# Attention with stationary values and per-head 64-row scores, in a fused attention and two-layer MLP kernel

## The chip, the cores and the metric

The kernel runs on one core of a Trainium2 chip. The metric is the device time of one execution in microseconds (us), as the median of several runs. A core has TensorE (PE, matrix products into PSUM), VectorE (DVE), ScalarE (ACT), GpSimd (POOL) and SyncE (SP, which issues the DMAs). Each works through its own queue in order and waits there on semaphores. PSUM has eight banks of 512 fp32 numbers per partition.

## The reference

For 8 batches and 8 heads, 576 queries of 64 numbers meet 72 keys and values, each the mean of 8 neighbours. Then come two layers on 4608 tokens.

```python
def _attn_ref(q, k, v):
    k_p = k.reshape(B, H, Sp, pool, D).mean(axis=3)
    v_p = v.reshape(B, H, Sp, pool, D).mean(axis=3)
    scores = scale * np.matmul(q, k_p.transpose(0, 1, 3, 2))
    scores = scores - np.max(scores, axis=-1, keepdims=True)
    attn = np.exp(scores)
    attn = attn / (np.sum(attn, axis=-1, keepdims=True) + 1e-09)
    return np.matmul(attn, v_p)

def _moe_ref(x, w_in, w_out, g_ln):      # 512 -> 1024 -> 512
    h = x @ w_in
    solu = h * softmax(h)
    ln = (solu - mean(solu)) / np.sqrt(var(solu) + 1e-06) * g_ln
    return ln @ w_out

def _moe2_ref(x, w_in, w_out):           # 512 -> 2048 -> 512
    h = x @ w_in
    g = h * (1.0 / (1.0 + np.exp(-1.702 * h)))
    return g @ w_out
```

## The kernel before

The program has two parts. The first computes the attention and the first layer for 36 tiles of 128 tokens, and meanwhile turns the weights of the second layer into sums of blocks in fp16, which go to DRAM. The second part computes the second layer in 12 blocks of 384 tokens with a seven-product scheme; the change leaves it as it is.

In the first part every piece of work is a Python generator that yields operations: `keys` and `values` (per batch), `attention` (per tile), `Pair.hidden` (per tile), `Pair.norm` and `Pair.project` (per pair of tiles), `Quarter.run` and `unit_scale` (second-layer weights). A planner (`Plan.run`) keeps an estimate of when each engine is free, asks every generator for its next operation, and emits the one with the earliest start, shifted a little by due times. So the order on each engine is fixed when the program is built, and it moves when an operation's estimated cost (`cost`, `T`, `X`), a buffer count or the operations change. An operation made with `VG` may go to POOL or DVE; the planner prefers POOL until DVE would be done over 3 us earlier. All operations of this part are recorded at L470 (engines), L491 (DMAs), L499 (products) and L514 (transposes on PE); their tiles tell them apart.

One tile of `attention` goes as follows. `qt` comes in with two heads stacked in its 128 partitions, in four pairs. The scores of a pair are one fp32 product of `qt` with `kbd`, in which the keys of the two heads stand in diagonal blocks with zeros beside them (144 columns); `keys` scales them into it from `kp`. In the records an fp32 product is two passes on PE. The eight heads' scores lie in two banks, `psx`. DVE takes the maxima (`mx`) and subtracts them (`e`); ACT takes exp. ACT and then POOL write `e` as fp16 high part and remainder into `st`, and a transposing DMA gives `aT`. The product with the values has `aT` as stationary operand and streams 65 columns of `vst`: a column of ones and the 64 values of a head, so it gives the sum of the exponentials as well. DVE adds 1e-9, takes the reciprocal (`rs`) and scales the result into `x`. PE transposes `x` in four products (L514), and ACT and DVE write the high part and the remainder of that into `xT`.

`psx` is one buffer of two banks: scores, value products, transposes and some of the spreads of a maximum over partitions (`largest`) take turns in it. `psh` (hidden products, two buffers of two banks) and `psy` (projections, two buffers of one bank) fill the other six. A tile of 128 tokens that straddles two batches has its products in two parts of 64 tokens.

`Pair.norm` takes small DVE operations on 128x2 numbers (`q`, `v`, `a`) around one POOL operation (`r`), then writes `zs`, which a transposing DMA turns into `zT` for `project`, whose result goes through ACT (`y`) to DRAM.

Of the kernel before, what the change touches and what calls it, by code (L numbers as in the profile page):

```python
# [8 lines left out]
F32 = mybir.dt.float32  # L9
# [3 lines left out]
ALU = mybir.AluOpType  # L13
# [18 lines left out]
VW = D + 1  # L32
PAD = 16
VP = P + PAD
# [42 lines left out]
V_TOP = 2.0 ** 14  # L77
LN_UP = 2.0 ** 10
# [198 lines left out]
def moe_kernel(ctx: ExitStack, tc: tile.TileContext, qT, kT, vT, w_in, w_out, g_ln, w2_in, w2_out, eye, outT):  # L277
# [135 lines left out]
    with ExitStack() as ph:  # L413
# [7 lines left out]
        psy = ph.enter_context(tc.tile_pool(name="psy", bufs=2, space=PSUM))  # L421
# [3 lines left out]
        vst = [wp.tile([P, H * VP + PAD], F16, name=f"vst{i}") for i in range(2)]  # L425
        kbd = [wp.tile([P, NPAIR, 2 * SP], F32, name=f"kbd{i}") for i in range(2)]
# [69 lines left out]
        def T(products):  # L496
# [9 lines left out]
            c = sum(count(p[2]) * 0.417 + 3 if p[2].dtype == F16 else count(p[2]) * 1.667 + 6 for p in products)  # L506
# [17 lines left out]
        def largest(am, alln, least, early=True):  # L524
# [8 lines left out]
            if early:  # L533
                ps = yield New(psy, [P, 2, YB], F32, "psy", "psy", 2)
            else:
                ps = yield New(psx, [P, 2, 512], F32, "psx", "psx")
            yield T([(ps[:, 0, :P], ones, diag, True, True)])
            drop(diag)
            yield V("tensor_reduce", out=alln, in_=ps[:, 0, :P], axis=AX.X, op=ALU.max)
# [207 lines left out]
        def pooled(kind, b, src, due):  # L747
            yield lambda: b == 0 or begun[kind][b - 1] == 2
            dst = yield New(kv, [P, NPAIR, SP], F32, kind + "p", bufs=1)
            yield until(*[start(half(kind, b, j, src, dst), due + j) for j in range(2)])  # L750
            return dst
# [12 lines left out]

        def values(b, due):
            vp = yield from pooled("v", b, vT, due)
# [15 lines left out]
            yield D(  # L782
                vst[b % 2][:, 0 : H * VP].rearrange("p (g w) -> p g w", w=VP)[:, :, PAD:VP], vx.rearrange("p a k -> p (a k)"),
                turn=True,
            )
# [17 lines left out]
        def attention(t):  # L803
# [5 lines left out]
            if t < 2:  # L809
# [3 lines left out]
            yield there(qt, *(kbd[b % 2] for _, _, b in spans(t)))  # L813
# [11 lines left out]
                    for o, n, b in spans(t)  # L825
                ]
# [7 lines left out]
            if plan.free["act"] + ACT_SPARE < plan.free["dve"]:  # L834
                for h in range(H):
                    yield A(out=e[:, h], in_=s4[:, h // 4, h % 4], func=AF.Exp, bias=mx[:, h : h + 1])
                drop(ps)
            else:
# [5 lines left out]
                yield A(out=e, in_=e, func=AF.Exp)  # L844
# [13 lines left out]
            x = yield New(sb, [P, DM], F32, "x", bufs=2)  # L858
            ps = yield New(psx, [P, 2, 512], F32, "psx", "psx")
            def v_at(h, c):  # L860
                return (h // 2 * 2 + c) * VP + PAD - 1 + h % 2 * VW

            p4 = ps.rearrange("p b (a c) -> p (b a) c", a=2)
# [3 lines left out]
                        p4[o : o + n, h // 2, (h % 2) * VW : (h % 2 + 1) * VW],  # L867
# [617 lines left out]
```

## Time and profile before

| what | value |
|---|---|
| time, median of 3 runs (lowest, highest) | 1304.92 us (1303.19, 1305.73) |
| profiled execution: its own time, its span | 1300.56 us, 1298.8 us |
| busy over the span: PE, DVE, ACT, POOL | 89%, 64%, 56%, 47% |
| first part, up to the last `psy` product | 589.2 us |
| mean granted TensorE clock | 0.987 of full |

Busy time counts an instruction from its start to its end on the engine, with what it waits for there after it has started. The 1.8 us between the span and the execution's own time lie outside the first and last instruction.

### The profile page before, as it was taken

Reading aid. Unit: us, or ns where it says so; the run is one execution under the profiler, and the core shown is the slowest. Engines: PE = TensorE matmul, PEld = TensorE weight load, DVE = VectorE, ACT = ScalarE, POOL = GpSimd, SP = SyncE. Lnnn points to the kernel's source line nnn. Section 1 sums busy time; section 2 is a strip of 40 time slices with the busy share of each in tenths; the row PEclk is TensorE's granted clock in tenths of the full one; section 3 lists DMA queues with packets and bytes.
Section 4 is the critical chain, followed back from the end, with each engine's and each line's share of the span. In section 5 each row is a group of like instructions: output and inputs, shape, how many; then the busy total and the mean of one; then the engine's idle time right before and its main releaser. Section 6 shows DMA issues by size and latency. Waiting matters only on the chain.

```text
span 1298.8 us, 27820 instructions
## 1 busy us (share of the span) xinstructions
PE 1160.4 (89%) x11822; PEld 1006.1 (77%) x11822; DVE 829.4 (64%) x1364; ACT 730.8 (56%) x961; POOL 606.8 (47%) x516
## 2 busy tenths in 40 slices
PE   2658878988889899989999999999999999999998
PEld 2334655666566667679999999999999999999998
DVE  8999989989889784424554637364554637273633
ACT  5578766767777775444453636354453636364543
POOL 5564577757775764323342426152332415252431
PEclk9969999999999999989999999999999999999999
DMA  9878899999979759557010101101010101101000
GB/s 306 243 211 185 206 241 264 223 243 245 252 200 217 174 126 256 182 98 268 14 38 15 36 26 32 44 8 44 14 38 14 38 26 29 47 7 44 12 16 26
DMA packets 246526, 152.88 MB, mean 118 GB/s; under 512 B 163585, under 2 KB 226177, under 8 KB 244097
## 3 DMA queue, kind: packets, MB, share of 16 engines
q1 hardware_dynamic: 246400, 151.09, 44.8%
q8 instruction: 93, 1.52, 0.5%
q14 instruction: 33, 0.26, 0.1%
HBM read 77.66 MB, written 33.55 MB: 86 GB/s over the span
## 4 chain that ended last, share of the span: by engine, by line
PE 26%; POOL 10%; DVE 9%; ACT 8%; issue 3%; DMA 0%; ACTq 0%; SPq 0%; POOLq 0%
PE bank_a L1295 17%; PE bank_d L1295 7%; DVE g L1342 6%; ACT w_g L1330 6%; POOL w_g L332 3%; POOL w_g L331 3%; POOL w_g L329 2%; PE bank_b L1295 2%; POOL w_g L330 2%; PE psy L499 1%; ACT g L1339 1%; DVE c L1308 1%; DVE w_g L329 1%; DVE w_g L330 1%; DVE w_g L331 0%
## 5 line engine op out<-in xcount | busy, mean ns | idle before, releaser
L1295 PEld LDWEIGHTS <-w2i 128*128 128x128 f16 x4032 | 334.2, 98 | 29.0 <-issue 28.9
L1295 PEld LDWEIGHTS <-w2o 128*128 128x128 f16 x4032 | 333.9, 98 | 8.8 <-issue 8.2
L1295 PE MATMUL bank_a<-ys,w2i 128*128 128x192 f16 x2304 | 213.7, 246 | 23.0 <-ACT c L1305 21.0
L329 POOL TENSOR_TENSOR w_g<-w_g 128x384 f32<-128x384 f32 x36 | 43.8, 1217 | 377.9 <-ACT w_g L1330 377.9
L499 PE MATMUL psh<-w1i,xT 128*128 128x512 f16 x864 | 206.3, 389 | 3.4 <-DVE mean L470 3.4
L1295 PE MATMUL bank_a<-g,w2o 128*128 128x192 f16 x2304 | 205.7, 246 | 1.2
L499 PE MATMUL psy<-zT,w1o 128*128 128x256 f16 x1728 | 198.9, 275 | 5.4 <-ACT tt L470 3.8
L499 PEld LDWEIGHTS <-w1o 128*128 128x128 f16 x1728 | 169.1, 99 | 27.0 <-issue 4.2
L1342 DVE SCALAR_TENSOR_TENSOR g<-w_g,gu_b,g 128x1152 f16<-128x1152 f32 (+1 forms) x96 | 168.1, 1772 | 25.4 <-ACT g L1339 25.3
L499 PEld LDWEIGHTS <-xT 128*128 128x128 f16 x864 | 85.0, 100 | 94.0 <-issue 11.8
L1305 ACT ACTIVATE c<-bank_a 128x384 f32<-128x384 f32 x192 | 91.5, 484 | 112.1 <-PE bank_a L1295 111.0
L1339 ACT ACTIVATE g<-w_g,gu_b 128x1152 f16<-128x1152 f32 (+1 forms) x96 | 132.9, 1407 | 38.2 <-POOL w_g L332 37.9
L1308 DVE SCALAR_TENSOR_TENSOR c<-bank_d,c 128x384 f32<-128x384 f32 x96 | 53.3, 555 | 132.3 <-ACT c L1305 97.8
L470 POOL TENSOR_TENSOR zs<-tt,zs 128x1024 f16<-128x1024 f32 x36 | 77.2, 2146 | 75.6 <-ACT zs L470 74.8
L1295 PE MATMUL bank_d<-g,w2o 128*128 128x192 f16 x1152 | 102.7, 246 | 3.6 <-DVE g L1342 3.6
L1295 PE MATMUL bank_d<-ys,w2i 128*128 128x192 f16 x1152 | 104.9, 246 | 0.0
L1330 ACT ACTIVATE w_g<-c,ch_b 128x1536 f32<-128x1536 f32 x48 | 75.3, 1568 | 37.0 <-DVE c L1308 36.9
L1305 ACT ACTIVATE c<-bank_a,co_b 128x384 f32<-128x384 f32 x47 | 26.8, 571 | 107.2 <-PE bank_a L1295 107.2
L499 PE MATMUL psx<-kbd,qt 128*128 128x144 f32 (+1 forms) x320 | 46.6, 307 | 25.5 <-DMA qt<-qT 12.3
L1308 DVE SCALAR_TENSOR_TENSOR c<-bank_b,c 128x384 f32<-128x384 f32 x48 | 26.7, 556 | 66.0 <-PE bank_b L1295 45.4
L470 POOL TENSOR_TENSOR lo<-w_f,hi 128x512 f16<-128x512 f32 (+1 forms) x47 | 63.6, 1366 | 7.2 <-DMA w2o_dram<-lo 4.0
L499 PEld LDWEIGHTS psx<-kbd,qt 128*128 128x128 f32 (+1 forms) x320 | 41.7, 194 | 31.8 <-DVE raw_z L470 12.3
(183 smaller groups left out, 1745.7 us busy)
## 6 DMA issues: line engine op xcount, KB each, us to landing
raw<-w_out SPq DMA_DIRECT2D x12, 1024.0 KB, 6.7
raw<-w_in SPq DMA_DIRECT2D x10, 1024.0 KB, 7.8
half<-kT SPq DMA_DIRECT2D x16, 576.0 KB, 5.3
half<-vT SPq DMA_DIRECT2D x16, 576.0 KB, 5.4
qt<-qT SPq DMA_DIRECT2D x36, 256.0 KB, 3.7
y_dram<-y SPq DMA_DIRECT2D x36, 256.0 KB, 2.7
y<-y_dram SPq DMA_DIRECT2D x48, 192.0 KB, 3.3
outT<-c SPq DMA_DIRECT2D x48, 192.0 KB, 1.9
```

The source lines that it names most:

```text
L329: eng.tensor_tensor(out=w[:, 1], in0=q[:, Q12], in1=q[:, Q11], op=ALU.subtract)
L330: eng.tensor_tensor(out=w[:, 2], in0=q[:, Q22], in1=w[:, 1], op=ALU.subtract)
L331: eng.tensor_tensor(out=w[:, 0], in0=q[:, Q22], in1=q[:, Q12], op=ALU.subtract)
L332: eng.tensor_tensor(out=w[:, 3], in0=q[:, Q21], in1=w[:, 2], op=ALU.subtract)
L470: getattr(eng, name)(*args, **kw)
L499: nc.tensor.matmul(*p[:3], start=p[3], stop=p[4])
L1295: nc.tensor.matmul(bank[:, q], self.weight(p, q, kk, w), self.data(p, kk, i), start=(first and q == 0 and kk == 0 and w == 0 and i == 0), ...
L1305: nc.scalar.activation(out=self.c[:, i], in_=bank, func=AF.Copy, scale=self.scale)
L1308: nc.vector.scalar_tensor_tensor(out=self.c[:, i], in0=bank, scalar=self.scale, in1=self.c[:, i], op0=ALU.mult, op1=ALU.add)
L1330: nc.scalar.activation(out=self.w[:, 0:4], in_=self.c, func=AF.Gelu_apprx_sigmoid, scale=self.ch)
L1339: nc.scalar.activation(out=self.g[:, 0, s], in_=self.w[:, s], func=AF.Copy, scale=self.gu)
L1342: nc.vector.scalar_tensor_tensor(out=self.g[:, 1, s], in0=self.w[:, s], scalar=self.gu, in1=self.g[:, 0, s], op0=ALU.mult, op1=ALU.subtract,)
```

## The change

The scores no longer use diagonal keys. `keys` sums the pooled keys straight into two alternating tiles `kps`, unscaled, and the scale goes into the exponential. Each head's scores are a product of its own 64 partitions of `qt` and `kps` with 72 columns; even heads write the first bank of `psx`, odd heads the second. So there are 8 products of 72 columns where there were 4 of 144.

The normalisation moves ahead of the value product: DVE sums `e` over the keys, adds 1e-9 and scales by 2^-14, takes the reciprocal, and POOL or DVE multiplies `e` by it. The value product now has 64 columns of `vst` as stationary operand and streams the 128 tokens of `aT`; even heads fill partitions 0 to 63 of the result, odd heads 64 to 127, so that the result already stands transposed. `x`, its scaling from PSUM, and the four transposes on PE are gone, and so are the columns of ones and the padding of `vst`. `xT` is read from the new one-bank buffer `psv`, scaled by 2^-14. `psv` also takes the later spreads of `largest`. To make room, `psy` has one buffer instead of two. In the planner, a product on 64 partitions, or with 64 rows of moving data, counts half.

```diff
-        psy = ph.enter_context(tc.tile_pool(name="psy", bufs=2, space=PSUM))
+        psy = ph.enter_context(tc.tile_pool(name="psy", bufs=1, space=PSUM))
+        psv = ph.enter_context(tc.tile_pool(name="psv", bufs=1, space=PSUM))
...
-        vst = [wp.tile([P, H * VP + PAD], F16, name=f"vst{i}") for i in range(2)]
-        kbd = [wp.tile([P, NPAIR, 2 * SP], F32, name=f"kbd{i}") for i in range(2)]
+        vst = [wp.tile([P, H, P], F16, name=f"vst{i}") for i in range(2)]
+        kps = [wp.tile([P, NPAIR, SP], F32, name=f"kp{i}") for i in range(2)]
...
-            c = sum(count(p[2]) * 0.417 + 3 if p[2].dtype == F16 else count(p[2]) * 1.667 + 6 for p in products)
+            c = sum(
+                (count(p[2]) * 0.417 + 3 if p[2].dtype == F16 else count(p[2]) * 1.667 + 6)
+                * (0.5 if count(p[1]) == P // 2 else 1)
+                for p in products
+            )
...
         def keys(b, due):
-            kp = yield from pooled("k", b, kT, due)
+            yield lambda: b == 0 or begun["k"][b - 1] == 2
             yield lambda: b < 2 or scored[last_tile(b - 2)]
-            for j in range(2):
-                r = slice(j * D64, (j + 1) * D64)
-                yield V(
-                    "tensor_scalar_mul", kbd[b % 2][r, :, j * SP : (j + 1) * SP], kp[r],
-                    1.0 / (NPOOL * math.sqrt(D64)),
-                )
-            drop(kp)
+            yield from pooled("k", b, kT, kps[b % 2], due)
...
-                        ps[o : o + n, p // 2, (p % 2) * 2 * SP : (p % 2 + 1) * 2 * SP],
-                        qt[:, p, o : o + n],
-                        kbd[b % 2][:, p, :],
+                        ps[o : o + n, j, p * SP : (p + 1) * SP],
+                        qt[j * D64 : (j + 1) * D64, p, o : o + n],
+                        kps[b % 2][j * D64 : (j + 1) * D64, p, :],
...
                     for p in range(NPAIR)
                     for o, n, b in spans(t)
+                    for j in range(2)
...
-                yield A(out=e, in_=e, func=AF.Exp)
+                yield A(out=e, in_=e, func=AF.Exp, scale=SCORE)
+            rs = s1("rs", H)
+            yield V("tensor_reduce", out=rs, in_=e, axis=AX.X, op=ALU.add)
+            yield V("tensor_scalar", out=rs, in0=rs, scalar1=1e-9, scalar2=1.0 / A_TOP, op0=ALU.add, op1=ALU.mult)
+            yield V("reciprocal", rs, rs)
+            yield VG("tensor_tensor", out=e, in0=e, in1=rs.unsqueeze(2).to_broadcast([P, H, SP]), op=ALU.mult)
...
-            x = yield New(sb, [P, DM], F32, "x", bufs=2)
-            ps = yield New(psx, [P, 2, 512], F32, "psx", "psx")
+            ps = yield New(psv, [P, DM], F32, "psv", "psv")
...
-                        p4[o : o + n, h // 2, (h % 2) * VW : (h % 2 + 1) * VW],
-                        aT[:, 2 * h + c, o : o + n],
-                        vst[b % 2][:, v_at(h, c) : v_at(h, c) + VW],
+                        ps[h % 2 * D64 : (h % 2 + 1) * D64, h // 2 * P + o : h // 2 * P + o + n],
+                        vst[b % 2][:, h // 2 * 2 + c, h % 2 * D64 : (h % 2 + 1) * D64],
+                        aT[:, 2 * (h % 2 * NPAIR + h // 2) + c, o : o + n],
...
-            yield V("tensor_scalar_add", r3, sums, 1e-9)
-            yield V("reciprocal", rs, rs)
-            yield V(
-                "tensor_tensor", out=x.rearrange("p (a h d) -> p a h d", a=NPAIR, d=D64),
-                in0=p4[:, :, 1 : 1 + P].rearrange("p a (h d) -> p a h d", h=2),
-                in1=r3.unsqueeze(3).to_broadcast([P, NPAIR, 2, D64]), op=ALU.mult,
-            )
-            drop(ps)
             xT = yield New(sb, [P, 2 * KM, P], F16, "xT", bufs=2)
-            ps = yield New(psx, [P, 2, 512], F32, "psx", "psx")
-            yield X([(ps[:, 0, k * P : (k + 1) * P], x[:, k * P : (k + 1) * P]) for k in range(KM)])
-            drop(x)
-            turned_x = ps[:, 0].rearrange("p (k t) -> p k t", t=P)
-            yield A(out=xT[:, 0:KM], in_=turned_x, func=AF.Copy)
-            yield V("tensor_tensor", out=xT[:, KM:], in0=turned_x, in1=xT[:, 0:KM], op=ALU.subtract)
+            turned_x = ps.rearrange("p (k t) -> p k t", t=P)
+            yield A(out=xT[:, 0:KM], in_=turned_x, func=AF.Copy, scale=1.0 / A_TOP)
+            yield V(
+                "scalar_tensor_tensor", out=xT[:, KM:], in0=turned_x, scalar=1.0 / A_TOP, in1=xT[:, 0:KM],
+                op0=ALU.mult, op1=ALU.subtract,
+            )
```

The planner moves the order with it. On DVE, in the stretch in which the hidden products run and the second-layer weights begin to come in, the order before is this (`tt` and `mean` belong to `hidden`, `q` and `v` to `norm`, `rs` and `x` to `attention`):

```order
L470 TENSOR_TENSOR xT<-psx,xT 128x512
L470 TENSOR_REDUCE w2a_129<-w2am 128x1
L470 ISA tt,mean<-psh,he 128x1024
L470 ISA mean 128x1
L470 TENSOR_SCALAR rs<-psx 128x8
L470 RECIPROCAL rs<-rs 128x8
L470 TENSOR_TENSOR x<-psx,rs 128x512
L470 TENSOR_SCALAR mean<-mean 128x1
```

In the changed kernel, at a like place, it is this:

```order
L470 TENSOR_REDUCE mx<-psx 128x8
L470 TENSOR_REDUCE rs<-e 128x8
L470 TENSOR_TENSOR e<-psx,mx 128x576
L470 TENSOR_SCALAR rs<-rs 128x8
L470 ISA tt,mean<-psh,he 128x1024
L470 ISA mean 128x1
L470 RECIPROCAL rs<-rs 128x8
L470 TENSOR_SCALAR mean<-mean 128x1
```

The work on `rs` has moved from behind the value product, where it read PSUM, to the exponentials in SBUF, and `x` is gone.

On POOL, where the first second-layer weights are combined (`w_f`, `lo`), the order before is this (`st` is the remainder of `e`, `zs` that of the normalised hidden row):

```order
L470 TENSOR_TENSOR w_f<-sg,raw 128x512 x2
L470 TENSOR_TENSOR r<-v,half_power 128x2
L470 TENSOR_TENSOR w_f<-w_f 128x256 x4
L470 TENSOR_TENSOR lo<-w_f,hi 128x512
L470 TENSOR_TENSOR lo<-w_f,hi 128x768
L470 TENSOR_TENSOR st_121<-e,st_121 128x8x72
L470 TENSOR_TENSOR lo<-w_f,hi 128x2x256
```

In the changed kernel it is this:

```order
L470 TENSOR_TENSOR zs<-tt,zs 128x1024
L470 TENSOR_TENSOR lo<-w_f,hi 128x2x256
L470 TENSOR_TENSOR e<-e,rs 128x576
L470 TENSOR_TENSOR zs<-tt,zs 128x1024
L470 TENSOR_TENSOR st_123<-e,st_123 128x8x72
L470 TENSOR_TENSOR r<-v,half_power 128x2
L470 TENSOR_TENSOR e<-e,rs 128x576
```

A product `e<-e,rs` has come into the queue for nearly every tile: 33 on POOL and 3 on DVE. Of the 36 differences `st`, DVE now has 4 and POOL 32, and three operations on second-layer weights that stood on DVE (one `lo`, two `w_f`) stand on POOL.

## Rows read from the trace of the kernel before

**Rows 1.** Busy time by stretch: PE, PEld, DVE, ACT, POOL, clock, DMA share, GB/s

```profile
45.00:130.00 85.00, 61.78 (x394) 34.48 (x393) 82.21 (x154) 62.93 (x93) 45.46 (x41) 0.86 0.85 224
130.00:390.00 260.00, 223.70 (x1825) 159.47 (x1824) 234.20 (x443) 183.55 (x262) 182.67 (x169) 0.99 0.98 234
390.00:480.00 90.00, 85.19 (x680) 59.53 (x679) 73.88 (x151) 64.63 (x90) 56.65 (x53) 1.00 0.73 169
480.00:549.00 69.00, 65.75 (x497) 45.51 (x495) 31.72 (x68) 36.14 (x52) 29.57 (x25) 1.00 0.89 228
...
sum 590.00, PE 482.78 PEld 338.69 DVE 470.36 ACT 387.17 POOL 347.45; mean PE 80.46 PEld 56.45 DVE 78.39 ACT 64.53 POOL 57.91
```

**Rows 2.** Waits from 130 to 390 us: total, times, longest

```profile
PE psx L499 <- DVE xT L470: 8.9, 7, 2.7
...
DVE q L470 <- POOL r L470: 6.9, 6, 2.3
```

**Rows 3.** Chain that ended last, end of the first part: start, duration, what

```profile
571.82 0.61 ACT y L470
...
572.90 5.63 DMA zT<-zs
...
578.57 10.65 PE psy L499 x96
589.23 0.82 PE bank_a L1295 x10
```

**Rows 4.** Groups of instructions up to 580 us: busy us, mean ns, idle before

```profile
L470 POOL TENSOR_TENSOR st<-e,st 128x576 f16<-128x576 f32 x36 | 47.5, 1319 | 40.3 <-ACT st L470 35.8 <-DMA vst<-vx 4.5
...
L470 DVE TENSOR_REDUCE mx<-psx 128x8 f32<-128x576 f32 x36 | 26.9, 747 | 4.5 <-PE psx L499 4.5
...
L470 DVE TENSOR_TENSOR x<-psx,rs 128x512 f32<-128x512 f32 x36 | 24.9, 692 | 1.1
...
L470 DVE TENSOR_SCALAR kbd<-kp 64x288 f32<-64x288 f32 x16 | 10.1, 634 | 0.1
...
L470 DVE TENSOR_SCALAR rs<-psx 128x8 f32<-128x8 f32 x36 | 5.6, 156 | 3.0 <-PE psx L499 3.0
...
L470 DVE TENSOR_TENSOR w_f<-w_f 128x256 f32<-128x256 f32 x2 | 2.8, 1381 | 0.4 <-POOL w_f L470 0.4
```

**Rows 5.** Two DVE operations: their groups, and min/median/max ns of each tile

```profile
L470 DVE TENSOR_SCALAR raw<-raw 128x512 int32<-128x512 int32 x44 | 39.9, 925 | 0.0
...
L470 DVE SCALAR_TENSOR_TENSOR q<-hsm,h_sc 128x2 f32<-128x2 f32 x18 | 10.7, 597 | 0.0
...
L470 DVE TENSOR_SCALAR raw<-raw x44: 408/467/8012, 26.1 to 443.7; 128x512 int32<-128x512 int32 x44
...
L470 DVE SCALAR_TENSOR_TENSOR q<-hsm,h_sc x18: 150/302/2096, 96.0 to 556.4; 128x2 f32<-128x2 f32 x18
```

**Rows 6.** Timeline of DVE and of POOL around 31 to 39 us

```profile
31.11 8.35 DVE L470 TENSOR_SCALAR raw<-raw 128x512 int32<-128x512 int32 x2
...
36.58 2.25 POOL L470 TENSOR_TENSOR w1i<-val,w1i 128x512 f16<-128x512 f32 x2
```

**Rows 7.** Timeline of PE: start, duration with the pipeline's tail, what

```profile
255.91 0.66 PE L499 MATMUL psx<-vst,aT 128*128 128x65 f16 x16
256.41 2.78 PE L499 MATMUL psy<-zT,w1o 128*128 128x256 f16 x24
259.55 0.63 PE L514 MATMUL psx<-eye_t,x 128*128 128x128 f32 x4 [0.36 <-DVE x L470]
260.01 8.02 PE L499 MATMUL psy<-zT,w1o 128*128 128x256 f16 x72
267.87 1.15 PE L499 MATMUL psx<-kbd,qt 128*128 128x144 f32 x8
268.86 1.46 PE L499 MATMUL psh<-w1i,xT 128*128 128x512 f16 x6
...
62.70 1.20 PE L499 MATMUL psx<-kbd,qt 128*64 128x144 f32 x16
```

More of the change, by code (lines that the diff above doesn't have):

```diff
@@ L77 @@
 V_TOP = 2.0 ** 14
+SCORE = 1.0 / (NPOOL * math.sqrt(D))
+A_TOP = 2.0 ** 14
 LN_UP = 2.0 ** 10
@@ L533, in largest @@
             if early:
-                ps = yield New(psy, [P, 2, YB], F32, "psy", "psy", 2)
+                ps = yield New(psy, [P, 2, YB], F32, "psy", "psy")
             else:
-                ps = yield New(psx, [P, 2, 512], F32, "psx", "psx")
-            yield T([(ps[:, 0, :P], ones, diag, True, True)])
+                ps = yield New(psv, [P, DM], F32, "psv", "psv")
+            spread = ps[:, 0, :P] if early else ps[:, :P]
+            yield T([(spread, ones, diag, True, True)])
             drop(diag)
-            yield V("tensor_reduce", out=alln, in_=ps[:, 0, :P], axis=AX.X, op=ALU.max)
+            yield V("tensor_reduce", out=alln, in_=spread, axis=AX.X, op=ALU.max)
             drop(ps)
@@ L781, in values @@
             yield lambda: b < 2 or valued[last_tile(b - 2)]
-            yield D(
-                vst[b % 2][:, 0 : H * VP].rearrange("p (g w) -> p g w", w=VP)[:, :, PAD:VP], vx.rearrange("p a k -> p (a k)"),
-                turn=True,
-            )
+            yield D(vst[b % 2], vx.rearrange("p a k -> p (a k)"), turn=True)
             v_ready[b] = True
@@ L812, in attention @@
             e = yield New(sb, [P, H, SP], F32, "e", bufs=2)
-            yield there(qt, *(kbd[b % 2] for _, _, b in spans(t)))
+            yield there(qt, *(kps[b % 2] for _, _, b in spans(t)))
             ps = yield New(psx, [P, 2, 512], F32, "psx", "psx")
@@ L834, in attention @@
             if plan.free["act"] + ACT_SPARE < plan.free["dve"]:
+                yield V("tensor_scalar_mul", mx, mx, SCORE)
                 for h in range(H):
-                    yield A(out=e[:, h], in_=s4[:, h // 4, h % 4], func=AF.Exp, bias=mx[:, h : h + 1])
+                    yield A(out=e[:, h], in_=s4[:, h // 4, h % 4], func=AF.Exp, bias=mx[:, h : h + 1], scale=SCORE)
                 drop(ps)
@@ L857, in attention @@
             yield there(aT, *(vst[b % 2] for _, _, b in spans(t)))
[L858 to L863 removed]
+            ps = yield New(psv, [P, DM], F32, "psv", "psv")
             yield T(
@@ L872, in attention @@
                     )
-                    for h in range(H)
+                    for p in range(NPAIR)
                     for o, n, b in spans(t)
                     for c in range(2)
+                    for h in (2 * p, 2 * p + 1)
                 ]
@@ L997, in project @@
                 yield there(self.zT, *w1o)
-                ps = yield New(psy, [P, 2, YB], F32, "psy", "psy", 2)
+                ps = yield New(psy, [P, 2, YB], F32, "psy", "psy")
                 for q in range(2):
@@ L1174, in clear @@
                 yield G("memset", minus_half, -0.5)
-            yield on("memset", kbd[i], 0.0)
             yield on("memset", st[i], 0.0)
@@ L1178, in clear @@
                 yield G("memset", vx[:, :, 3 * SP :], 0.0)
-            for col in (PAD - 1, VP):
-                v = vst[i][:, col : col + (H - 1) * VP + 1 : VP].rearrange("p (a c) -> p a c", c=2)
-                yield on("memset", v[:, :, 0], 1.0)
-                yield on("memset", v[:, :, 1], 0.0)
-                yield on("memset", v[0 : 2 * SP - P, :, 1], 1.0)
         def eye_load():
```

18 lines of the change are left out of this document (5 added, 13 removed).

## Prediction

> **What bounds the kernel now.** I read the profile from the outside in: the page, then a table of busy time by stretch, then who waits for whom, then single rows. The page's shares in the table above, 64% for VectorE (DVE) and 89% for TensorE (PE), are averages of two halves that have different limits. The second half, from 589 us on, is untouched by the change. [rows 1] split the first. From 45 to 390 us DVE is busy 82.2 of 85 and 234.2 of 260 us, while PE has 223.7 of 260: DVE is the limit. [rows 2] say the same from the other side: what PE waits for there is DVE, and DVE's longest wait for another engine is 6.9 us in 260, for GpSimd's (POOL's) `r`. From 390 to 549 us it turns round: PE is busy 85.2 of 90 and 65.8 of 69, DVE 31.7 of the last 69. After the last hidden product the end is latency: [rows 3] follow the last pair of tiles through a transposing DMA of 5.63 us into 10.65 us of `psy` products, which end at 589.2 and let the second half begin. So an edit is paid by what it does to DVE until about 430 us (by my estimate 30 of the 36 tiles' attention), to PE in the last tiles, and to the last pair's chain.
>
> **The change part by part, DVE.** Taken away, from [rows 4]: `x<-psx,rs` 24.9 us, the sum with 1e-9 from PSUM 5.6 us, and the 16 scalings into `kbd` 10.1 us, together 40.6. The order also takes 6.2 us from DVE: one subtraction of the maxima (0.8, priced as the maximum) and three weight operations that go to POOL (the two `w_f` at 2.8 and one `lo` that I price like two of these, 2.6). Removed: 46.8 us.
>
> Added: a sum over each head's 72 keys, 36 times. Its nearest row is the maximum over the same 128x576, 747 ns: 26.9 us. The sum's scaling, 36 small operations, 156 ns by the row of the one that they replace: 5.6 us. The reciprocal stays. The remainder `xT` now also scales, at 1 us in all by my estimate. Of the 36 products e x rs DVE gets 3, and of the `st` differences 4: seven operations of 128x576, between 0.75 us (the maximum's row, the same width out of PSUM) and 1.38 us each (`w_f` on DVE, both operands in SBUF): 5.3 to 9.7 us, and I take 9.7, since both operands here are in SBUF. So far 43.2 us: DVE would come out at 46.8 - 43.2 = 3.6 us less.
>
> **What POOL does to DVE.** This decides the sign. [rows 5] hold an operation of DVE on SBUF alone, `raw` by a scalar: fastest 408 ns, mean 925, once 8012. [rows 6] show that case: from 31.11 us two of them take 8.35 us, while POOL runs `w1i` and `st` without a gap to 38.8, and DVE is free half a microsecond later. The small `q<-hsm` (2 elements) takes 150 ns at best and 597 in the mean. The excess is 44 x 0.517 = 22.7 us and 18 x 0.447 = 8.0 us; operations that read PSUM, such as `x` and `mx`, show no such spread. The Trainium skill, page "SBUF — State Buffer", section "Who interferes with whom", has a rule for it: DVE shares a port pair with GpSimd, and an operation with two SBUF inputs, or a scalar one in a fast mode, blocks until the other engine's instruction is over. The trace agrees for these rows; by that rule a sum (one SBUF input) waits for nobody and the new scaling does. Without any lock the sum below would end some 15 us lower.
>
> Two terms follow. First, the new `rs` scaling reads SBUF where the old one read PSUM. Its lock wait lies between 0 (as `mx`, from PSUM) and 0.52 us (as `raw`); I take 0.3, between the two and near the 0.447 of `q<-hsm`: 36 x 0.3 = 10.8 us, ends 0 and 18.7. Second, POOL gets 33 products e x rs. The nearest row is `st`, 1.319 us for the same 576 columns: 43.5 us, less 4 `st` (5.3), and with 3.6 for the three weight operations 41.8 us more on 347 us of [rows 1]. The excess of those two families, 30.7 us on 347, would grow by 12%, 3.7 us; other DVE rows on SBUF suffer too, so I take 7, ends 0 and 10. Net on DVE: -3.6 + 10.8 + 7 = **+14.2 us**; the ends are -3.6 - 4.4 (seven operations at their lowest) = -8 and -3.6 + 18.7 + 10 = +25. About 30/36 of it falls before 430 us, +11.8 us. Some 3 us of that hides in waits that DVE has anyway, and POOL's longer queue ahead of `r` adds about 1 to the 6.9 us of [rows 2]. On the path: **+9.8 us**.
>
> **PE.** The starts of [rows 7] give what a tile costs in a full queue: 16 products with `vst` 0.50 us, 4 transposes 0.46, 8 score passes 0.99. The transposes go: -0.46 per tile. The scores become 16 passes of half the width on half the rows. If the two halves of the array work at once, 0.5 us, if not and each pass costs as now, 2.0. The straddling tile of [rows 7] runs 16 passes on halves of the columns in 1.20 us against 1.15 for 8 full ones, so halves do overlap there; I take 0.75. The value products stream 128 columns instead of 65 but in two column halves: 0.5, up to 1.0. So a tile saves 0.7 us of PE, ends +1.05 and -0.96. Up to 430 us DVE covers this either way. In the PE-bound stretch, by the order, some 8 tiles still have value products ahead and 5 their scores: 8 x 0.46 + 5 x 0.24 = **-4.9 us**, ends +5 and -6.
>
> The Trainium skill, page "TensorEngine Tiling (Array Packing)", section "Key Properties", says that changing the tiling mode drains the engine. No row of before isolates that. If each of four changes in a tile cost the tail of one product (0.66 - 0.50 = 0.16 us of [rows 7]), the saving of 0.7 us would be nearly gone, and the sum would be 5 us higher.
>
> **Banks and the end.** `psx` no longer serves three uses in turn, which ends PE waits such as the 8.9 us of [rows 2]; behind DVE that is worth nothing by itself. `psy` goes from two buffers to one: the second half of a pair must wait for ScalarE's copy, 0.61 us in [rows 3]. Between the halves the order puts other products at most places; in the last pair nothing, +0.7 us. There 24 products of the second half now stand before the last `psy` instead of 2; they fit into PE's wait for `zT`, and 22 x 0.082 us ([rows 3], 10 in 0.82) come off afterwards: -1.8. End: **-1.1 us**. The chain to `aT` grows by the sum, the scaling, the reciprocal and POOL's product, about 2.4 us; scores run three or more tiles ahead, so I cost it at nothing, except for the first tile: there it delays the first hidden product by 2 us, but before, DVE's 8.35 us stall of [rows 6] lay ahead of the same tile's `x`, so I leave the start at 0, ends -5 and +3.
>
> **Sum.** 9.8 - 4.9 - 1.1 = +3.8 us, rounded to +4. The profiled execution took 1300.56 us (span 1298.8), which gives 1304.6; the median of the three runs is 4.4 us higher, so I forecast **1309 us**.
>
> **Rivals.**
> *Freed engine* (faster): the lock waits stay near 0 because the scheduler's gaps fall well, DVE comes out at -8 us, 30/36 of it on the path is -7; PE gives -6, the end -1, the start -5 as the stall of [rows 6] is gone. Sum -19, some 1286; half of it, 1295, is the likelier size. With PE and end as forecast the sum is zero where the two lock terms fall from 17.8 to 13 us together. For it: DVE has nothing but these waits against it, and the margin is small. Against it: 925 ns in place of 408.
> *Cancelling* (no change): the lock terms come to some 13 us instead of 17.8, so DVE's cost on the path is about 6 us, and PE and the end take that back: 1305.
> *Array not split* (slower by more): passes run one after the other and mode changes cost, +5 in the last stretch instead of -4.9, so 1319. This is also the case in which the change does not do what it says.
> *POOL as the limit* (slower): POOL's 182.7 of 260 us in [rows 1] becomes about 203. The chain through e x rs, `st` and `zs` then queues behind weight work, and DVE waits for `r` and `xT`. At 0.4 us a tile that is another 14 us: 1323.
>
> **How the numbers follow.** A measurement of this kernel can tell about 0.2%, 2.6 us, from no change. Forecast 0.36, freed engine 0.33, cancelling 0.13, array not split 0.08, POOL as the limit 0.10. The forecast's own range is 1308 to 1317. Both signs are held by large cases, so the range goes from 1289 to 1325. Faster 0.33, same 0.13, slower 0.54.
>
> **What would show it.** In the new profile: DVE's busy time before the second half at or above 470 us in spite of 46.8 us removed; `rs<-rs` with a mean near 0.45 us and a fastest near 0.16; `e<-e,rs` on POOL at 1.3 us; scores of a tile in 0.5 to 1 us; no PE wait for `x`; the last pair's chain as in [rows 3]. I am wrong if `rs<-rs` stays at 0.16 us, or if DVE turns out to have idled for reasons that the new banks remove, so that its busy share between 130 and 390 us falls clearly under the 90% of [rows 1].

## The result and the profile after

The changed kernel takes 1315.58 us (median of 4 runs, 1312.08 to 1317.87) against 1304.06 us before: ratio 1.0086, 95% interval 1.0067 to 1.0106, 11.5 us slower. Some executions fall into a slower state of the chip, and all ratios leave these out. The forecast was 1309 us: right in sign and inside the range, but less than half of the size, and as the experiments show, for a reason that was mostly wrong.

The profiled execution took 1313.53 us (span 1311.7, mean granted clock 0.967 against 0.987). The loss divides at two points. After the last hidden product, PE's next row starts at 556.29 us (548.94 before): 7.35 us. From there to the first product of the second part behind the last `psy` it takes 44.2 us (556.29 to 600.52; before 548.94 to 589.06, 40.1): another 4.1. The last 1.4 of the 12.9 us between the spans come behind that point.

First the table of busy time by stretch, which answers to [rows 1], with the same columns:

```profile
45.00:130.00 85.00, 61.41 (x493) 34.67 (x491) 83.18 (x164) 64.44 (x96) 57.70 (x55) 0.84 0.90 219
130.00:390.00 260.00, 220.78 (x1825) 147.22 (x1823) 232.04 (x409) 174.33 (x251) 187.38 (x170) 0.93 0.87 218
390.00:480.00 90.00, 83.35 (x688) 54.40 (x685) 79.43 (x158) 65.12 (x92) 69.40 (x67) 0.94 0.79 198
480.00:549.00 69.00, 62.45 (x465) 40.63 (x462) 31.67 (x65) 37.83 (x58) 30.96 (x25) 0.96 0.81 220
```

DVE (third pair) is no busier than before from 130 to 390 us. PE (first pair) is less busy in every stretch, though its work got shorter only by the transposes, and its clock, the number behind POOL's pair, is lower in all of them (0.93 against 0.99 in the long one). In the long stretch PE stands still for 39.2 us against 36.3 before, so little more in all, but in longer pieces, the longest 6.6 us against 2.7; and 0.06 of clock on 220.8 busy us is, as an estimate from these rows, some 13 us of its work at full clock. PE's waits from 130 to 390 us, beside [rows 2]:

```profile
PE psv L499 <- DVE xT L470: 21.2, 9, 4.8
PE psv L499 <- DVE diag L470: 9.6, 3, 6.6
PE psy L499 <- ACT y L470: 3.8, 4, 2.3
```

All three are waits at the banks that the change put in place of the old ones. The longest of them on PE's timeline (start, duration, what, wait ahead of it in brackets), and on DVE's:

```profile
338.62 1.11 PE L499 MATMUL psx<-kp,qt 64*128 64x72 f32 x16
346.29 0.77 PE L499 MATMUL psv<-diag,ones 128*128 128x128 f32 x2 [6.56 <-DVE diag L470]
346.86 6.60 PE L499 MATMUL psy<-zT,w1o 128*128 128x256 f16 x48
```

```profile
343.22 0.67 DVE L470 SCALAR_TENSOR_TENSOR xT<-psv,xT 128x512 f16<-128x512 f32 x1
...
345.37 0.78 DVE L470 TENSOR_SCALAR diag<-eye_t,w2a 128x128 f32<-128x128 f32 x1
```

`largest` spreads a maximum through `psv`. DVE reads the value product's `psv` only at 343.22 and builds `diag` at 345.37; PE, which takes its queue in order, stands still until then with 48 `psy` products next in its queue. Those then take 6.60 us where 48 take 5.40 elsewhere, at a granted clock of 0.79 from 346.3 to 353.5 us, so the gap is paid twice.

The end of the first part, beside [rows 3]:

```profile
573.38 5.40 PE L499 MATMUL psy<-zT,w1o 128*128 128x256 f16 x48 [0.69 <-ACT y L470]
579.46 5.40 PE L499 MATMUL psy<-zT,w1o 128*128 128x256 f16 x48 [0.69 <-ACT y L470]
585.54 5.40 PE L499 MATMUL psy<-zT,w1o 128*128 128x256 f16 x48 [0.69 <-ACT y L470]
591.68 5.40 PE L499 MATMUL psy<-zT,w1o 128*128 128x256 f16 x48 [0.73 <-ACT y L470]
600.52 1.15 PE L1277 MATMUL bank_a<-ys,w2i 128*128 128x192 f16 x12 [3.44 <-ACT c L1287]
601.51 1.77 PE L1277 MATMUL bank_d<-ys,w2i 128*128 128x192 f16 x12
```

Before, the chain ran through the last `zT`; now it alternates between a half of the projection and ScalarE's (ACT's) copy of it. Behind the last half stands a new wait of 3.44 us, for ACT's copy `c` of `bank_a`. ACT's own queue there:

```profile
597.16 0.60 ACT L470 ACTIVATE y<-psy 128x512 f32<-128x512 f32 x1 [5.54 <-PE psy L499]
599.98 0.49 ACT L1287 ACTIVATE c<-bank_a 128x384 f32<-128x384 f32 x1 [2.22 <-DMA y_dram<-y]
```

`bank_a` had been full since before 567 us, but `c` stands behind the last `y` in ACT's queue, and ACT waits 2.22 us more between the two. The chain that ended last shows for what:

```profile
597.16 0.61 ACT y L470
597.79 2.09 DMA y_dram<-y
...
599.98 0.50 ACT c L1287
```

So most of the 3.44 us is the transfer of the last `y` to DRAM. In the kernel before, `c` waits for no such transfer and starts 0.23 us behind `y`:

```profile
590.14 0.49 ACT L1305 ACTIVATE c<-bank_a 128x384 f32<-128x384 f32 x1 [0.23 <-PE bank_a L1295]
```

After the gap the clock falls, which the same table over 600 to 607 us shows (0.76; before it is 1.00 there), and 12 products take 1.77 us instead of 1.15:

```profile
600.00:607.00 7.00, 6.48 (x59) 6.31 (x59) 1.12 (x2) 1.95 (x4) 0.00 (x0) 0.76 0.97 341
```

Last, the operations that the prediction priced (groups as in [rows 4], then min/median/max ns as in [rows 5]):

```profile
L470 POOL TENSOR_TENSOR e<-e,rs 128x576 f32<-128x576 f32 x33 | 39.9, 1210 | 31.7 <-DVE rs L470 17.9 <-DVE q L470 5.9 <-DVE mean L470 5.7
L470 DVE TENSOR_SCALAR raw<-raw 128x512 int32<-128x512 int32 x44 | 33.5, 782 | 0.0
L470 DVE TENSOR_REDUCE rs<-e 128x8 f32<-128x576 f32 x36 | 26.8, 743 | 1.3 <-ACT e L470 1.3
L470 DVE TENSOR_SCALAR rs<-rs 128x8 f32<-128x8 f32 x36 | 14.0, 390 | 0.4
```

```profile
L470 DVE TENSOR_SCALAR rs<-rs x36: 150/170/1674, 22.1 to 491.0; 128x8 f32<-128x8 f32 x36
...
L470 DVE TENSOR_SCALAR raw<-raw x44: 375/437/1709, 26.1 to 445.3; 128x512 int32<-128x512 int32 x44
```

### The profile page after: what moved, and what is told of

Same layout as the page of the kernel before. It is cut to its first block, busy times and chain, and to the rows that moved or that the text cites. A ratio compares the mean times of both kernels' runs of the same rounds, so it can differ in the third digit from the quotient of the medians.

```text
span 1311.7 us, 28155 instructions
## 1 busy us (share of the span) xinstructions
PE 1166.3 (89%) x11998; PEld 993.4 (76%) x11998; DVE 833.8 (64%) x1346; ACT 729.3 (56%) x968; POOL 641.9 (49%) x541
## 3 DMA queue, kind: packets, MB, share of 16 engines
q1 hardware_dynamic: 246400, 151.09, 42.6%
## 4 chain that ended last, share of the span: by engine, by line
PE 28%; POOL 10%; DVE 8%; ACT 8%; issue 3%; DMA 0%; ACTq 0%
PE bank_a L1277 17%; PE bank_d L1277 7%; ACT w_g L1312 6%; DVE g L1324 5%; POOL w_g L331 3%; POOL w_g L330 3%; POOL w_g L328 2%; PE bank_b L1277 2%; PE psy L499 2%; POOL w_g L329 2%; ACT g L1321 1%; DVE c L1290 1%; DVE w_g L328 0%; DVE w_g L329 0%; ACT c L1287 0%
## 5 line engine op out<-in xcount | busy, mean ns | idle before, releaser
L499 PE MATMUL psh<-w1i,xT 128*128 128x512 f16 x864 | 216.6, 406 | 14.9 <-DVE mean L470 13.1
L499 PE MATMUL psy<-zT,w1o 128*128 128x256 f16 x1728 | 204.6, 278 | 12.6 <-ACT y L470 11.5
L499 PEld LDWEIGHTS <-w1o 128*128 128x128 f16 x1728 | 171.3, 100 | 43.5 <-issue 14.2
L1287 ACT ACTIVATE c<-bank_a,co_b 128x384 f32<-128x384 f32 x47 | 26.9, 572 | 107.2 <-PE bank_a L1277 107.2
L470 DVE TENSOR_REDUCE hmx<-psh 128x1 f32<-128x1024 f32 x36 | 43.7, 1214 | 46.7 <-PE psh L499 46.7
L499 PE MATMUL psx<-kp,qt 64*128 64x72 f32 (+1 forms) x640 | 44.0, 294 | 29.2 <-issue 12.4
```

The costliest lines, as they stand in the source:

```text
L470: getattr(eng, name)(*args, **kw)
L499: nc.tensor.matmul(*p[:3], start=p[3], stop=p[4])
L1287: nc.scalar.activation(out=self.c[:, i], in_=bank, func=AF.Copy, scale=self.scale)
```

## The experiments

Three explanations stood against each other. *DVE*: the normalisation on `e` costs DVE time, as the prediction has it. *Banks*: `psy` with one buffer, and `psv` shared by value products and spreads, make PE wait. *Order*: the planner writes another order for every edit, and orders differ. All runs in one table; a ratio is to the kernel before, on the same chip. "Hidden" is where PE's last hidden product ends (start of its next row, or the end by the trace where PE waits next), "second" the start of the first product behind the last `psy`, both in us of the profiled run, which is one execution and up to 10 us from its kernel's median (e2 1314.89 us, e3 1300.33). "To bank_d" is the time from "hidden" to the first `bank_d` product of the second part: in every kernel the same 36 products of the second part stand ahead of that one, while ahead of "second" there are none to 2 with two `psy` buffers and 24 with one.

| kernel | ratio (95%) | hidden | second | between | to bank_d | `psy` buffers | late spreads |
|---|---|---|---|---|---|---|---|
| before | 1 | 548.9 | 589.1 | 40.1 | 42.9 | 2 | psx |
| e9, before, other order | 1.0038 (1.0019 to 1.0057) | 558.9 | 597.0 | 38.0 | 40.8 | 2 | psx |
| e1, scores part alone | 0.9925 (0.9893 to 0.9957) | 538.7 | 576.6 | 37.9 | 42.6 | 2 | psx |
| e3, changed, old banks | 0.9930 (0.9908 to 0.9953) | 540.4 | 581.0 | 40.6 | 45.1 | 2 | psx |
| e4, before, one `psy` | 1.0034 (1.0007 to 1.0060) | 550.0 | 595.3 | 45.4 | 46.6 | 1 | psx |
| changed | 1.0086 (1.0067 to 1.0106) | 556.3 | 600.5 | 44.2 | 45.2 | 1 | psv |
| e8, changed, other order | 0.9992 (0.9969 to 1.0016) | 546.7 | 591.4 | 44.7 | 46.2 | 1 | psv |
| e11, changed, third order | 1.0119 (1.0073 to 1.0165) | 553.7 | 600.8 | 47.1 | 49.0 | 1 | psv |
| e2, changed, diagonal keys | 1.0012 (0.9987 to 1.0037) | 554.8 | 599.5 | 44.7 | 46.6 | 1 | psv |
| e7, changed, no scaling | 1.0051 (1.0029 to 1.0074) | 552.1 | 596.3 | 44.2 | 45.2 | 1 | psv |
| e5, changed, `psy` in halves | 0.9994 (0.9970 to 1.0019) | 537.8 | 587.7 | 49.9 | 50.8 | 2 halves | psv |
| e6, changed, spreads in psx | 0.9913 (0.9886 to 0.9940) | 532.1 | 576.3 | 44.3 | 45.3 | 1 | psx |
| e10, e6 with the number of e8 | 0.9948 (0.9920 to 0.9977) | 536.1 | 580.1 | 44.0 | 45.2 | 1 | psx |
| e12, e6, no scaling | 0.9966 (0.9944 to 0.9989) | 540.4 | 584.7 | 44.3 | 46.2 | 1 | psx |

### e1 and e2: the two parts apart

e1 is the kernel before with the scores part alone:

```diff
-                        ps[o : o + n, p // 2, (p % 2) * 2 * SP : (p % 2 + 1) * 2 * SP],
-                        qt[:, p, o : o + n],
-                        kbd[b % 2][:, p, :],
+                        ps[o : o + n, j, p * SP : (p + 1) * SP],
+                        qt[j * D64 : (j + 1) * D64, p, o : o + n],
+                        kps[b % 2][j * D64 : (j + 1) * D64, p, :],
```

> The kernel before with the scores part of the change alone: pooled keys unscaled and without diagonal blocks, scale in the exponential, each head's scores from its own 64 partitions, even and odd heads in two banks; value product, transposes of x and banks as before. DVE theory (the bound up to 430 us is DVE, 16 scalings into kbd are 10.1 us): about 10.1 x 30/36 = 8 us come off, some 1296. Rival, no gain: PE's score passes take as long as the diagonal ones (1.04 to 1.05 us a tile in the changed kernel against 0.99), and what DVE gains is lost in waits for PE or banks: 1302 to 1306. Rival, PE loses: 16 passes of 64 rows need more than 8 of 128, +0.06 x 36 = 2 us and a lower clock: 1306 to 1309.

Measured: 1294.66 us, ratio 0.9925, 9.8 us off (5.6 to 14.0 by the interval). The saving of 8 us on DVE came, or something of its size; one order of the planner's can't tell which (e8 to e11).

e2 is the changed kernel with these lines, the scaling of keys and the diagonal blocks put back.

> The changed kernel with the diagonal keys put back: stationary values, normalisation ahead of the value product and the new banks stay; scores as before. If the parts add up and the scores part gives 8 us, this is 1315.6 + 8 = 1323 or so. If the scores part gives nothing, 1315 to 1317. If the scores part is what costs (slower passes on PE), it comes out below the changed kernel, 1308 to 1313.

Measured: 1305.25 us, ratio 1.0012, below all three branches. Taking the part away that saves 8 us did not cost 8 us, and by the third branch the scores part would be what costs, which e1 speaks against. The parts do not add up; e8 shows why this alone says little.

### e3 and e4: the banks

e3 is the changed kernel with the banks of before:

```diff
-        psy = ph.enter_context(tc.tile_pool(name="psy", bufs=1, space=PSUM))
-        psv = ph.enter_context(tc.tile_pool(name="psv", bufs=1, space=PSUM))
+        psy = ph.enter_context(tc.tile_pool(name="psy", bufs=2, space=PSUM))
...
-            ps = yield New(psv, [P, DM], F32, "psv", "psv")
+            both = yield New(psx, [P, 2, 512], F32, "psx", "psx")
+            ps = both[:, 0]
```

> The changed kernel with the banks of before: psy has two buffers again, and value products and the later spreads go back into psx; psv is gone. Bank theory: the five waits of 0.7 us for ScalarE's copy of psy and the 3.4 us one behind them in the last 45 us go (some 5 us), and so do the 21.2 + 9.6 us of PE's waits for psv, of which a part was on the path: 1303 to 1310. DVE theory: waits for banks only move, and psx in three uses brings back its own 8.9 us of waits: 1313 to 1317.

Measured: 1295.68 us, ratio 0.9930, beyond what even the bank theory expected. It has the whole arithmetic of the change and the time of e1, which has only the scores part, although up to the mark "second" DVE is busy for 466.9 us here and 451.1 in e1. So in these two orders those 15.8 us of DVE cost nothing that shows.

e4 is the kernel before with one buffer for `psy` (`bufs=2` becomes `bufs=1` in its pool, and the same in its requests; nothing uses the bank that comes free).

> The kernel before with one buffer for psy in place of two, nothing else (a bank stays empty). Bank theory: half-pairs that stand one behind the other at the end wait 0.7 us each for ScalarE's copy, and the planner shifts others: before + 3 to 6 us, 1307 to 1310. The prediction's price: +0.7 us in the last pair, 1304 to 1306.

Measured: 1310.47 us, ratio 1.0034, 4.4 us slower (0.9 to 7.8), at the upper end of the bank theory's branch. In total that is no more than another order alone does to this kernel (e9, 1.0038), so the price has to be read from the end. PE's timeline at its end of the first part:

```profile
573.41 5.40 PE L499 MATMUL psy<-zT,w1o 128*128 128x256 f16 x48 [0.69 <-ACT y L470]
580.26 5.41 PE L499 MATMUL psy<-zT,w1o 128*128 128x256 f16 x48 [1.46 <-DMA zT<-zs]
586.41 5.40 PE L499 MATMUL psy<-zT,w1o 128*128 128x256 f16 x48 [0.73 <-ACT y L470]
595.33 1.48 PE L1295 MATMUL bank_a<-ys,w2i 128*128 128x192 f16 x12 [3.52 <-ACT c L1305]
```

The same alternation, and the same wait for `c`, as in the changed kernel, without anything else of the change. With two buffers, in e3:

```profile
570.48 10.65 PE L498 MATMUL psy<-zT,w1o 128*128 128x256 f16 x96 [0.98 <-DMA zT<-zs]
580.97 1.15 PE L1277 MATMUL bank_a<-ys,w2i 128*128 128x192 f16 x12
581.96 1.15 PE L1277 MATMUL bank_b<-ys,w2i 128*128 128x192 f16 x12
584.58 1.15 PE L1277 MATMUL bank_a<-ys,w2i 128*128 128x192 f16 x12 [1.46 <-DMA y<-y_dram]
```

Both halves run as one block of 96, and 24 products of the second part follow them, which cover part of ACT's wait. The wait is here too, although `psy` has two buffers:

```profile
584.03 0.49 ACT L1287 ACTIVATE c<-bank_a 128x384 f32<-128x384 f32 x1 [2.22 <-DMA y_dram<-y]
```

Of the 14 kernels 12 have this wait of 2.2 to 2.4 us for `y_dram<-y`, e1 with its two buffers among them; only before and e9 have 0.23 us. So it comes with the order or the rest of the edit, not with the single `psy`; why is open. What the single `psy` adds is the alternation, 0.69 to 0.73 us a half, and it stands with an order that leaves nothing to cover the wait for `c`.

In the table the column "between" holds 37.9 to 40.6 us for the four kernels with two buffers and 44.0 to 47.1 for the nine with a single whole one, but that mark flatters two buffers: with them, the first products of the second part come behind it, and so does PE's wait (1.72 us for `c` in e1, 1.46 in e3, which ends as `c` does). To `bank_d` it is 40.8 to 45.1 and 45.2 to 49.0 us, 3.3 us apart in the mean, and 3.7 from before to e4; the changed kernel and e3 are level, though e3 has a wait of 5.43 us for a `diag` in that stretch. So the end with one buffer is longer by some 3 us, with the size open.

### e5 and e6: which of the banks

e5 uses `psy`'s one bank as two halves in turn, so that ACT copies one while PE fills the other:

```diff
-                ps = yield New(psy, [P, 2, YB], F32, "psy", "psy")
                 for q in range(2):
                     m = 2 * half + q
+                    yield lambda: not taken[q]
+                    taken[q] = True
...
-                                ps[:, q],
+                                bank_y[:, q],
...
+                    yield A(out=y[:, q], in_=bank_y[:, q], func=AF.Copy)
+                    taken[q] = False
```

> The changed kernel with psy's one bank used as two halves of 256 columns in turn: a half of the projection is copied by ScalarE while PE fills the other one. psv stays as it is. If the single psy is what cost (psy waits of 0.7 us a half, 11.5 us in all over the first part, and the lower clock behind them), most of the 20 us that the banks of before gave back comes back here too: 1297 to 1305. If psy is worth what it is worth in the kernel before (4.5 us) and the rest is psv, 1309 to 1312. DVE theory: no change, 1313 to 1317.

Measured: 1300.67 us, ratio 0.9994. By the total it is the first branch, by the trace it is not: the end between the two marks got longer (49.9 us), PE still waits 21.0 us for `y` from 45 to 549 us, and what it won lies ahead of the last hidden product. The halves did not do what they were for, so this run prices nothing.

e6 gives `psv` to value products alone:

```diff
             else:
-                ps = yield New(psv, [P, DM], F32, "psv", "psv")
-            spread = ps[:, 0, :P] if early else ps[:, :P]
+                ps = yield New(psx, [P, 2, 512], F32, "psx", "psx")
+            spread = ps[:, 0, :P]
```

> The changed kernel with the later spreads of largest in psx again, so that psv holds value products alone; psy stays single. If the waits of value products for a spread's diag (9.6 us from 130 to 390 us, longest 6.6) were on the path: 1303 to 1310. If they only stood in for other waits: 1313 to 1317. Sum of this run's gain and that of the half banks should come near the 20 us of the banks of before, if the two terms are all of it.

Measured: 1290.63 us, ratio 0.9913, the fastest of all, below both branches and by the ratios 22.6 us below the changed kernel. With the 12.0 of e5 that makes 34.6, not the 20 of e3: the gains do not add up. PE's waits from 130 to 390 us are now

```profile
PE psv L499 <- DVE xT L470: 22.0, 11, 8.7
PE psy L499 <- ACT y L470: 5.1, 5, 1.6
PE psx L499 <- DVE e L470: 1.7, 2, 1.5
```

The waits for `diag` are gone; those of value products for `xT` have stayed. The end still takes 44.3 us: the single `psy` is still paid for.

### e7 and e12: DVE work taken away

```diff
-            yield V("tensor_scalar", out=rs, in0=rs, scalar1=1e-9, scalar2=1.0 / A_TOP, op0=ALU.add, op1=ALU.mult)
...
-A_TOP = 2.0 ** 14
+A_TOP = 1.0
```

e7 is this edit in the changed kernel, e12 in e6.

> The changed kernel without the scaling of rs (adding 1e-9 to a sum that is at least 1 leaves it in fp32, and the factor 2^14 is left out at both ends): 36 operations of 390 ns in the mean, 14.0 us, go from DVE; everything else stays. DVE theory: 14.0 x 30/36 = 11.7 us come off, some 1304. Bank theory: DVE only fills waits here, 0 to 4 us come off, 1312 to 1316.

> The changed kernel with the later spreads in psx and without the scaling of rs (adding 1e-9 does nothing in fp32, the factor 2^14 is left out at both ends). The version that should beat both. DVE theory: 13.5 us of DVE work go, 11 of them from the time: 1280. If DVE only fills waits: within luck of the order of 1290.6, that is 1285 to 1296.

Measured: e7 1308.96 us, 1.0051 against 1.0086, 4.6 us off; e12 1299.80 us, 0.9966 against 0.9913, 6.9 us *on*, outside what either theory expected. Together, about +1 us. Busy time from 45 to 430 us, of e6 and then of e12 (columns as in [rows 1]):

```profile
45.00:430.00 385.00, 323.70 (x2747) 213.33 (x2746) 360.43 (x677) 281.50 (x408) 296.43 (x277) 0.94 0.95 229
```

```profile
45.00:430.00 385.00, 322.86 (x2664) 208.49 (x2664) 350.17 (x634) 278.77 (x408) 291.70 (x270) 0.92 0.93 227
```

DVE is busy 10.3 us less in e12, and PE and POOL are no busier for it. But e10, which has the scaling and differs from e6 only in the planner's number (next section), has DVE busy there for 352.8 us, 7.6 less than e6, so this row can't be put down to the scaling. That 11.7 us come off with it did not show in either run; with orders as far apart as the next runs have them, two runs don't exclude that a part of it is there.

### e8 to e11: what an order is worth

```diff
-HASTE = 0.01
+HASTE = 0.0105
```

This number weighs due times in the planner. It changes no operation, only the order, and by it the engine of a few `VG` operations (DVE takes none of the 36 products `e<-e,rs` in e6, one in e10). e8 is the changed kernel with it, e11 with 0.0095, e9 the kernel before with 0.0105, e10 is e6 with 0.0105.

> The changed kernel with one number of the planner moved by 5% (the weight of due times, 0.01 to 0.0105): the same instructions in another order. It measures how much of the difference between two plans is luck of the order. If differences of some us are causes: within 2 us of the changed kernel, 1314 to 1318. If luck of the order is worth 5 us or more, this run lies outside 1310 to 1320.

> The kernel before with the same one number of the planner moved by 5% (0.01 to 0.0105). The same step took 13 us from the changed kernel, so the order is worth that much there. If the order of before is just as open to luck: outside 1300 to 1310. If the kernel before is less so: within 3 us of it, and the two kernels with this number differ by less than 3 us.

> The run with the later spreads of largest back in psx, with the planner's number at 0.0105. At 0.01 it stood 25 us below the changed kernel. If psv's double use is the cause of a good part of that, this run lies clearly below the changed kernel with the same number (1302): 1288 to 1296. If it was luck of the order: 1298 to 1306.

> The changed kernel with the planner's number at 0.0095. A third order of the same instructions: 1316 and 1302 are known. If 1316 is an unlucky order: 1298 to 1308. If 1302 is a lucky one: 1312 to 1320. The end of the first part, psy with one buffer, should in either case take 44 to 45 us from the last hidden product to the first product of the second part's own stretch, as in all orders with one buffer so far.

Measured: e8 1302.16 us (0.9992), e11 1316.94 (1.0119), so three orders of the changed kernel lie 1.3% apart; e11 lies in the branch by which 1302 was a lucky order (and its end takes 47.1 us, not the 44 to 45 expected). e9 came out at 1308.40 (1.0038), between its branches: before, too, moves, by less in the one step tried. The difference between e8 and e9 is 0.46%, 6 us the other way from the result. Means over the orders are 1.0066 for the changed kernel (three) and 1.0019 for before (two): some 6 us, with single orders up to 10 us from their mean, so five orders can't tell this difference from none. The measured 11.5 us are those of one pair of orders.

e10 is the check on e6: 1296.76 us, ratio 0.9948, 0.8 us above the branch for a cause, and still below e8, though the two intervals just overlap. Three pairs differ in the spreads alone: changed and e6 (1.0086, 0.9913), e8 and e10 (0.9992, 0.9948), e7 and e12 (1.0051, 0.9966): -22.6, -5.7 and -11.1 us, -13 in the mean. The last hidden product is earlier in all three, by 24.2, 10.6 and 11.7 us. PE's waits for a spread in `psv` (`diag`, `w2all`) from 45 to 549 us are 11.5, 13.7 and 5.4 us in the changed kernel, e8 and e7, and none in the other three. All three pairs and these waits point the same way; but each edit also changes the order, and orders alone differ by as much, so the sign is well supported and not proven, and the size is open between 6 and 23.

## The prediction, point by point

**DVE as the limit up to 430 us: wrong step.** The working turned each microsecond of DVE into 30/36 of one on the path. DVE's own measured growth, +3.7 us (next point), would by that rule be about +1 on the path (30/36 of it, less 3 that hide, plus 1 behind POOL), not +9.8, and the measured loss is 11.5. Nor did taking work away bring the rule's price: e7 and e12 took 14.0 and 13.5 us of DVE work away for -4.6 and +6.9 us, and e3 has 15.8 us more than e1 at the same ratio. What the trace shows in place of this step is PE's waits at `psv`, 30.8 us from 130 to 390 us (before, 36.3 at `psx` in shorter ones), and with the longer ones a lower granted clock, 0.93 against 0.99. No run separates the waits from the clock. A busy share of 90% [rows 1] did not mean that DVE's work sets the pace: DVE reads banks that PE fills, PE waits for banks that DVE empties, and what is taken from one turns into waiting of the other. e1 alone fits the rule (8 expected, 9.8 measured), in one order. The signs that the working named mostly came true (DVE busy for over 470 us, `rs<-rs` at 0.39 us, `e<-e,rs` at 1.21, DVE at 89% from 130 to 390 us): they show that its terms exist, not that they lie on the path.

**DVE's own sum: terms right, one sign wrong.** The new sum took 26.8 us (26.9 said), products and differences that DVE kept 9.0 (4.7 + 4.3; 9.7 said), the scaling 14.0 (5.6 + 10.8 = 16.4 said). The wait of that scaling behind POOL is as forecast: 150 ns at best and 390 in the mean on SBUF, where the same operation on PSUM before had 156 [rows 4] and never over 168. Eight of the twelve that took over 0.35 us end 20 to 40 ns behind an instruction of POOL, the longest with `zs`, which POOL began before it:

```profile
207.61 1.67 DVE L470 TENSOR_SCALAR rs<-rs 128x8 f32<-128x8 f32 x1
...
207.12 2.14 POOL L470 TENSOR_TENSOR zs<-tt,zs 128x1024 f16<-128x1024 f32 x1
```

The Trainium skill, page "SBUF — State Buffer", section "Who interferes with whom", says that an operation of DVE in a two-port mode, which a scalar one can enter, and an instruction of GpSimd exclude each other for the whole instruction, and the trace agrees. But that other operations would suffer too, +7 us, was mis-sized: `raw` by a scalar fell from 39.9 us [rows 5] to 33.5, since the single stall of 8.0 us did not come again (longest now 1.709), with 34 us more work on POOL up to 602 us (381.5 against 347.5). In all DVE was busy 474.1 us up to 602 us against 470.4 up to 590 before: +3.7 where +14.2 was forecast.

**PE: half right.** The transposes went. Scores were to take 0.75 us and take 1.04, value products 0.5 and take 0.57 (starts below). (The ends for a tile are slightly off: the working's own terms give +0.95 and -1.05, not +1.05 and -0.96.) PE's waits grew by more than the products got shorter, so PE is less busy in the late stretches, 83.35 and 62.45 us against 85.19 and 65.75 [rows 1], and -4.9 us did not come.

**Banks and end: mis-sized, and one bank overlooked.** -1.1 us was said. The end costs +4.1 (+2.3 to `bank_d`), and 1.4 more is lost behind it, where the clock is lower. Two sentences of that part failed. "Between the halves the order puts other products at most places; in the last pair nothing, +0.7": five halves stand in a row at the end and wait 0.69 to 1.53 us each. "22 products come off afterwards, -1.8": they did, but they had stood where PE now waits 3.44 us for `c`, and 2.1 us of that is a transfer of `y` that no term of the working had. e4, without the rest of the change, has the same alternation and the same wait. The shared `psv` was not priced at all; the text counts only the `psx` waits that end and calls them worth nothing. Three pairs put 6 to 23 us there, with the order mixed in. The order, listed before the run, showed both: 240 `psy` products in a row, and spreads between the value products.

**The chain of the last pair** was to stay as in [rows 3]; it went from `zT` to the alternation of `psy` and `y`.

**Rivals.** *Array not split* has its passes right but for the straddling tiles, and not their effect: e1 has them and is faster. *POOL as the limit* is out: 187.4 us of 260, not 203, and in e6, the fastest run, it is 206.6. *Freed engine* gave the size that e6, e3 and e10 have, 1286 to 1295 against 1290.6 to 1296.8, not by its mechanism: the scaling in e6 still takes 375 ns in the mean. So the sum of +4 got the sign of +11.5 by luck: DVE was charged for what the banks did, and another order of the same kernel (e8, 0.9992) has no loss at all.

**Open.** What sets the pace up to 430 us when the banks are free. DVE is busy 239.7, 241.1 and 241.0 of 260 us from 130 to 390 us in e6, e10 and e12, more than before, so it may be near its limit there. And how much of e1's 9.8 us is its order.

## What to carry to other kernels

Count what each PSUM bank serves after a change, and for each use what the next one in the queue waits for; a bank that two kinds of work share, or that loses its second buffer, can cost in an in-order queue what no sum of busy times shows. Products that follow a block may be the cover of another engine's step: before they are moved ahead, look who needed the time, and what else (here a transfer) that step waits for. Compare ends of a stretch at a point behind the same amount of work. And where a planner writes the order, time two or three orders of both kernels before a difference of 1% is given a cause.

## What the runs showed of the hardware

Row halves of the array gave nothing where a product uses all 128 columns. PE's starts in the changed kernel, scores and value products with the row behind each:

```profile
260.65 1.11 PE L499 MATMUL psx<-kp,qt 64*128 64x72 f32 x16
261.69 1.47 PE L499 MATMUL psh<-w1i,xT 128*128 128x512 f16 x6
...
278.84 0.73 PE L499 MATMUL psx<-kp,qt 64*64 64x72 f32 x32 [0.67 <-PE psy L499]
279.50 1.47 PE L499 MATMUL psh<-w1i,xT 128*128 128x512 f16 x6
...
297.30 0.64 PE L499 MATMUL psv<-aT,vst 128*64 128x128 f16 x16 [2.87 <-DVE xT L470]
297.87 2.56 PE L499 MATMUL psh<-w1i,xT 128*128 128x512 f16 x6
```

16 score passes of 72 columns on 64 rows take 1.04 us, 65 ns each; 8 passes of 144 on all rows took 0.99 [rows 7], 124 ns each: nearly the same time per column (0.90 and 0.86 ns), as if the two halves took turns, though they write two banks. In a straddling tile it is otherwise: 32 passes on 64 rows and 64 columns take 0.66 us, where 16 passes on all rows and 64 columns took about 1.13 before (1.20 with the tail [rows 7]). The Trainium skill, page "TensorEngine Tiling (Array Packing)", section "Theoretical Speedup", has up to twice the speed for a dimension of 64; for the rows this case shows it, at 1.7 times, only in straddling tiles (three of four; the first, from 49.35 us, takes 1.17 us at a lower granted clock). Column halves do overlap: 128 columns on half of the array take 0.57 / 16 = 36 ns, where 256 columns on the whole one take 7.86 / 72 = 109 by the starts of [rows 7].

A gap of PE can cost more than its length, and not every time: after 6.56 us of waiting 48 products took 6.60 us instead of 5.40; around the 3.44 us ahead of the second part the granted clock was 0.76 from 600 to 607 us in the changed kernel, and behind a gap of the same 3.44 us it was 0.57 from 584.6 to 591.6 us in e12 and 1.00 from 576 to 583 us in e6.
